# A gated linear attention with two MLPs: one prefix scan for all heads of a chunk, contiguous transposed copies, and part of the weight split on TensorE

## The chip, the cores and the metric

The kernel runs on one core of a Trainium2 chip. The metric is the device time of one launch in microseconds (us); three runs of the kernel before gave 1174.3, 1174.88 and 1174.89 us, median 1174.88. The profiled execution took 1172.15 us, of which the trace's span is 1170.1 us.

## The reference

A complex-valued recurrence per batch (4), head (8) and position (768), head size 48, then two MLPs over the 3072 tokens, everything in fp32:

```python
mag = np.sqrt(a_re * a_re + a_im * a_im)
scale = np.minimum(mag, 0.999) / (mag + 1e-06)
a_re_n, a_im_n = a_re * scale, a_im * scale
for t in range(S):
    ar, ai = a_re_n[:, :, t, :, None], a_im_n[:, :, t, :, None]
    new_re = ar * S_re - ai * S_im
    new_im = ar * S_im + ai * S_re
    S_re, S_im = new_re + np.einsum('bhd,bhe->bhde', k[:, :, t], v[:, :, t]), new_im
    y[:, :, t] = np.einsum('bhd,bhde->bhe', q[:, :, t], S_re)
x = y.transpose(0, 2, 1, 3).reshape(3072, 384)
x = np.maximum(x @ w_in, 0.0) ** 2 @ w_out                 # w_in 384x2048, w_out 2048x384
g = x @ w_gate
out = (g / (1 + np.exp(-g)) * (x @ w_val)) @ w_out2        # 384x1536, 384x1536, 1536x384
```

## The kernel before

The sequence is cut into six chunks of 128 positions; with the batch of 4 a chunk has 512 tokens. For every chunk there are three pieces of work.

**Attention** (`attention`, `elem`, `mat`). The eight heads are four groups of two. `elem` works in the layout 128 partitions = 4 batches x 32 blocks of positions, each block of 4 positions (`nb`) in the free dimension. It loads the decays (`load`, names `in2`, shown as `in`), normalises them with Ln and Exp on ScalarE (`sq`, `lg`, `b0`, `z`), and forms running complex products on VectorE: within a block of 4 (`an`, through the scratch `AB`), then over the 32 blocks by a five-level scan in a transposed copy `X`. The result `gb` multiplies `an` to give the prefix products `pp` (scratch `Bt`). With them q and k are scaled to `qs` and `ks`. All of this runs once for each pair of groups (`m`, twice a chunk). `mat` transposes `ks` and `qs` on TensorE into PSUM (`pt`), copies them to `kT`, `qT` with ScalarE, makes scores (`sc`), masks them (`pb`), applies them to v (`py`) and updates the `state` (`pu`, `rho`). `pt` is written in contiguous runs; the copy to `kT`/`qT` puts elements 4 apart.

**First MLP** (`moe1`): 16 steps, each 9 matmuls into `h` and, two steps later, 9 into `acc`; an fp32 number is the sum of two fp32r numbers, and each product is three matmuls (high times high, high times low, low times high). ScalarE makes `u` and `gh`, VectorE makes `gl`. **Second MLP** (`moe2`): 12 steps a chunk with `pg`, `pv`, `acc`, after all chunks of the first.

**Weights.** `prep1` loads 32 tiles of `w_in` and `w_out`, `prep2` 36 tiles of the second MLP (`wst`). `wsplit` builds the fp32 value with three VectorE instructions (`wt`), ScalarE casts the high part (`wc`, `wr`), VectorE subtracts to get the low part, and ScalarE takes two checks of the original bits (`wst<-wst`).

**Order.** All calls between `constants` and `issue` go through `Plan`: `record` keeps each call with its dependences, `arrange` runs a list schedule with estimated durations (`weigh`), in which the rank of an instruction is its place in the recorded program, and `issue` emits the calls in that order on the five in-order engines. So every instruction shows the line of one helper in the profile, and groups are told apart by tile names. `fast` sets the recorded order: attention of chunk 0 first, then `moe1` of chunk n interleaved with the attention of chunk n+1 (`drain`, weights `NATT`), with `prep1` run between the steps of `moe1(0)` (`behind`).

Of the kernel before, what the change touches and what calls it, by code (L numbers as in the profile page):

```python
# [22 lines left out]
class Op:  # L23
    __slots__ = ("call", "args", "kw", "engine", "step", "last", "after", "order", "users", "need", "frees", "tiles", "rank",
                 "ready", "pair", "size")
# [13 lines left out]
class Plan:  # L39
# [9 lines left out]
    def __init__(self, tc):  # L49
        self.tc, nc = tc, tc.nc  # L50
        self.ops, self.seen, self.slots, self.tags = [], {}, {}, {}
        for name in ("tensor", "vector", "scalar", "sync", "gpsimd"):
            setattr(self, name, Engine(self, getattr(nc, name), name))

    @staticmethod
    def region(ap):
        (row, parts), free = ap.ap[0], ap.ap[1:]
        if ap.space == bass.MemoryType.DRAM:
            return 0, 1, ap.offset, ap.offset + sum(st * (n - 1) for st, n in ap.ap) + 1
        p, f = divmod(ap.offset, row)  # L60
        return p, p + parts, f, f + sum(st * (n - 1) for st, n in free) + 1
# [8 lines left out]
    def record(self, engine, method, call, args, kw):  # L70
# [4 lines left out]
        o = Op()  # L75
        i = len(self.ops)
        o.call, o.args, o.kw, o.engine, o.rank = call, args, kw, engine, i
        o.after, o.order, o.users, o.frees, o.tiles, o.ready, o.pair, o.size = set(), set(), [], [], [], 0.0, None, 0
        self.ops.append(o)
        for k, ap in aps.items():  # L80
# [11 lines left out]
            for j, r, w in t[1]:  # L92
                if (write or w) and j != i and r[0] < at[1] and at[0] < r[1] and r[2] < at[3] and at[2] < r[3]:
                    same = self.ops[j].engine == engine and engine != "sync"
# [4 lines left out]
                    if write and at[0] <= r[0] and r[1] <= at[1] and at[2] <= r[2] and r[3] <= at[3] and j not in o.order:  # L99
                        continue  # L100
# [10 lines left out]
    def weigh(self, engine, method, full, aps):  # L111

        out = aps["out"]
        n = self.width(out)
        if engine == "vector":
# [26 lines left out]
        parts = out.ap[0][1] if out.space != bass.MemoryType.DRAM else aps["in_"].ap[0][1]  # L142
        free = out if out.space != bass.MemoryType.DRAM else aps["in_"]
        return 470, 2000 + 4 * parts * self.width(free) / 200.0


    def arrange(self):
# [38 lines left out]
        while len(result) < n:  # L186
# [45 lines left out]
            if e == "tensor":  # L232
# [9 lines left out]
                if o.pair and lastpair and o.pair[0] == lastpair[0] and o.pair[1] != lastpair[1]:  # L242
                    now[e] -= 0
                    step *= 0.06
                lastpair = o.pair
                acc += step
            if e in ("sync", "gpsimd"):
# [34 lines left out]
class Kern:  # L282
    CHUNKS = None

    NIN = 3
    NPP = 3
# [7 lines left out]
    NATT = 150  # L294
# [6 lines left out]
    READ = 8  # L301

    LOADS = 5
# [3 lines left out]
    def __init__(self, tc, q, k, v, a_re, a_im, w1, w2, wg, wv, wo, out):  # L307
# [8 lines left out]
        self.G, self.SG = 2, 2  # L316
# [3 lines left out]
        for nb in self.CHUNKS or [4] * (self.S // 128):  # L320
            self.chunks.append((t, nb))
            t += 32 * nb
# [3 lines left out]
    def pools(self, ctx):  # L326
# [11 lines left out]
        self.wbufs, self.wlive, self.wspare = self.WBUFS, 0, []  # L338
        self.x2, self.in2 = {}, {}

    def constants(self, ctx):
# [28 lines left out]
        self.ytile = c.tile([128, self.SG * W // 32, 32], F32, name="ytile")  # L370
        nc.vector.memset(self.ytile, 0.0)

    def flags(self, pool):
# [8 lines left out]
        self.low = pool.tile([128, n * NG // self.SG, self.SG * self.G * self.D // 32], F32, name="low")  # L382
# [34 lines left out]
    def load(self, n, g, names):  # L417
# [4 lines left out]
        t = self.ld.tile([128, 2, G, nb * D], F32, name="in2", tag="in2", bufs=self.NIN)  # L422
# [14 lines left out]

    def cmul(self, o, x, y, AB):

        nc = self.nc  # L440
        w = list(x.shape[2:])
        nc.vector.tensor_tensor(out=AB, in0=x.unsqueeze(1).to_broadcast([128, 2, 2] + w),
                                in1=y.unsqueeze(2).to_broadcast([128, 2, 2] + w), op=ALU.mult)
# [3 lines left out]
    def elem(self, n, m, res):  # L447

        nc, G, D, W, SG = self.nc, self.G, self.D, self.W, self.SG
        t0, nb = self.chunks[n]  # L450
        NG = self.H // G
        VW = SG * W
        big = lambda nm: self.e2.tile([128, 2, nb, W], F32, name=nm, tag="pp", bufs=self.NPP)
        smn = lambda nm: self.e2.tile([128, nb, W], F32, name=nm, tag="smn", bufs=self.NSMN)
        sml = lambda nm: self.e2.tile([128, nb, W], F32, name=nm, tag="smk", bufs=self.NSMK)
        cs = lambda nm, shape: self.e2.tile(shape, F32, name=nm, tag="cs", bufs=6)
        perm = lambda t: t.rearrange("p h (r d) -> p r h d", r=nb)
        v4 = lambda t: t.rearrange("p r (h d) -> p r h d", h=G)
        an = self.e2.tile([128, 2, nb, VW], F32, name="an", tag="an", bufs=1)
        part = lambda i: an[:, :, :, i * W:i * W + W]  # L460

        for i in range(SG):
            a2 = self.load(n, m * SG + i, (self.a_re, self.a_im))
            sq = [smn(f"sq{c}") for c in range(2)]
# [5 lines left out]
            lg = smn("lg")  # L470
# [3 lines left out]
            b0 = smn("b0")  # L474
# [11 lines left out]
            for c in range(2):  # L486
                nc.vector.tensor_tensor(out=v4(part(i)[:, c]), in0=perm(a2[:, c]), in1=v4(sc), op=ALU.mult)
# [8 lines left out]
        X = self.e2.tile([128, 2 * K * 32 + 32], F32, name="X", tag="X", bufs=1)  # L496
        X4 = lambda t: t.rearrange("p (c k j) -> p c k j", c=2, k=K)
        bs = slice(m * K, (m + 1) * K)
        for c in range(2):
            nc.vector.transpose(out=X[:, 32 * K * c + 1:32 * K * (c + 1) + 1], in_=an[:, c, nb - 1])  # L500
        t31 = cs("t31", [128, 2, K])
        nc.vector.tensor_copy(t31, X4(X[:, 32:])[:, :, :, 0])
# [597 lines left out]
```

## Time and profile before

| what | value |
| --- | --- |
| median of three runs | 1174.88 us |
| profiled execution | 1172.15 us |
| its span | 1170.1 us |
| TensorE busy (matmul) | 1054.8 us, 90% |
| VectorE busy | 728.9 us, 62% |
| ScalarE busy | 656.2 us, 56% |
| mean granted clock of TensorE | 0.972 |

Busy times are unions over the span; the launch takes 2.05 us more than the span. An engine's share says little here, since the kernel has three stages with different limits, so the stretches are read one by one.

### The profile page before, as it was taken

The numbers are of one execution on the slowest core, as the hardware profiler recorded it, in microseconds if no ns is written. First come the engines' busy times: TensorE is split into PE (matmuls) and PEld (weight loads), VectorE is DVE, ScalarE is ACT, GpSimd is POOL, SyncE is SP. The second block draws the span as 40 slices with busy tenths as digits, with TensorE's granted clock in tenths as the row PEclk, the third lists the DMA queues.
The fourth block names the chain that finished last, engine by engine and source line by source line (L and its number), as shares of the span: only waits on it lengthen the run. The fifth ranks groups of instructions, "written<-read, shape, count | busy, mean of one in ns | idle before, by whom it ended". The sixth has DMA issues, their size and how long they took to land.

```text
span 1170.1 us, 16337 instructions
## 1 busy us (share of the span) xinstructions
PE 1054.8 (90%) x5842; PEld 892.8 (76%) x5842; DVE 728.9 (62%) x1582; ACT 656.2 (56%) x1332; POOL 0.9 (0%) x7
## 2 busy tenths in 40 slices
PE   0527586989999999999999999999999999999997
PEld 0425465768888888888888788888888888888886
DVE  6998999798969879886886787522232222322221
ACT  2657687987678776777767998522122221311211
POOL 0000000000000000000000000000000000000000
PEclk9958897999999999999999999999999999999999
DMA  5426345223141432414224545110010010000000
GB/s 174 135 62 170 109 137 147 71 79 92 46 130 60 109 102 62 122 48 129 73 50 138 187 134 177 55 41 13 1 55 1 7 48 1 28 1 1 28 1 31
DMA packets 102490, 89.25 MB, mean 76 GB/s; under 512 B 35072, under 2 KB 90368, under 8 KB 102400
## 3 DMA queue, kind: packets, MB, share of 16 engines
q1 hardware_dynamic: 102400, 88.12, 25.6%
q8 instruction: 48, 0.79, 0.3%
q14 instruction: 42, 0.34, 0.1%
HBM read 64.49 MB, written 18.87 MB: 71 GB/s over the span
## 4 chain that ended last, share of the span: by engine, by line
PE 77%; ACT 10%; DVE 9%; issue 1%; DMA 1%; SPq 1%; DVEq 0%; ACTq 0%
PE acc L279 25%; PE pg L279 13%; PE pv L279 13%; PE h L279 12%; PE py L279 4%; PE pt L279 3%; PE sc L279 3%; ACT wst L279 3%; PE pu L279 3%; DVE AB L279 1%; ACT u L279 1%; DVE wt L279 1%; SPq L279 1%; DVE pp L279 1%; ACT gh L279 1%
## 5 line engine op out<-in xcount | busy, mean ns | idle before, releaser
L279 ACT CAST gh<-u 128x512 fp32r<-128x512 f32 x168 | 103.9, 619 | 220.2 <-PE acc L279 195.0
L279 PE MATMUL h<-xh,wc 128*128 128x512 f32 x576 | 203.5, 406 | 25.7 <-ACT wc L279 19.9
L279 PE MATMUL acc<-gh,wr 128*128 128x512 f32 x576 | 202.2, 406 | 6.9 <-ACT gh L279 6.9
L279 DVE TENSOR_TENSOR gl<-u,gh 128x512 fp32r<-128x512 f32 x168 | 115.7, 689 | 117.5 <-ACT gh L279 116.7
L279 DVE TENSOR_TENSOR u<-pv,u 128x512 f32<-128x512 f32 x72 | 49.7, 691 | 191.9 <-PE pv L279 189.6
L279 PEld LDWEIGHTS h<-xh,wc 128*128 128x128 f32 x576 | 109.2, 192 | 52.6 <-ACT wc L279 21.8
L279 PE MATMUL acc<-wr,gh 128*128 128x384 f32 x576 | 147.3, 336 | 0.0
L279 PE MATMUL pg<-xh,wc 128*128 128x512 f32 x432 | 145.9, 392 | 0.0
L279 PE MATMUL pv<-xh,wc 128*128 128x512 f32 x432 | 144.9, 390 | 0.0
L279 PEld LDWEIGHTS acc<-gh,wr 128*128 128x128 f32 x576 | 108.8, 192 | 30.6 <-ACT gh L279 9.6
L279 PE MATMUL h<-xl,wc 128*128 128x512 f32 x288 | 116.0, 403 | 2.2 <-DVE xl L279 2.2
L279 PE MATMUL acc<-gl,wr 128*128 128x512 f32 x288 | 115.6, 402 | 0.3 <-DVE gl L279 0.2
L279 PEld LDWEIGHTS acc<-wr,gh 128*128 128x128 f32 x576 | 105.6, 188 | 4.7
L279 ACT ACTIVATE u<-pg 128x512 f32<-128x512 f32 x72 | 43.0, 598 | 98.2 <-PE pg L279 97.6
L279 PE MATMUL acc<-wr,gl 128*128 128x384 f32 x288 | 97.1, 337 | 0.0
L279 PEld LDWEIGHTS pv<-xh,wc 128*128 128x128 f32 x432 | 81.2, 188 | 17.3
L279 PEld LDWEIGHTS pg<-xh,wc 128*128 128x128 f32 x432 | 81.2, 188 | 15.5
L279 PE MATMUL pt<-ident,ks 128*96 128x128 f32 x192 | 31.3, 288 | 64.5 <-DVE ks L279 63.5
L279 PE MATMUL pg<-xl,wc 128*128 128x512 f32 x216 | 85.1, 394 | 0.0
L279 PE MATMUL pv<-xl,wc 128*128 128x512 f32 x216 | 84.3, 390 | 0.0
L279 ACT ACTIVATE u<-h 128x512 f32<-128x512 f32 x96 | 57.1, 595 | 40.7 <-PE h L279 38.3
L279 PEld LDWEIGHTS pt<-ident,ks 128*96 128x96 f32 x192 | 22.9, 135 | 68.4 <-issue 64.4
(111 smaller groups left out, 1820.2 us busy)
## 6 DMA issues: line engine op xcount, KB each, us to landing
wst<-in_moe_w_out_dram SPq DMA_DIRECT2D x28, 384.0 KB, 3.5
scr<-ks SPq DMA_DIRECT2D x24, 384.0 KB, 2.6
kn<-scr SPq DMA_DIRECT2D x24, 384.0 KB, 3.7
wst<-in_moe_w_in_dram SPq DMA_DIRECT2D x16, 384.0 KB, 4.7
in<-in_a_re_dram SPq DMA_DIRECT2D x96, 48.0 KB, 1.9
in<-in_a_im_dram SPq DMA_DIRECT2D x96, 48.0 KB, 1.9
in<-in_k_dram SPq DMA_DIRECT2D x96, 48.0 KB, 2.8
in<-in_q_dram SPq DMA_DIRECT2D x96, 48.0 KB, 2.6
```

The costliest lines, as they stand in the source:

```text
L279: o.call(*o.args, **o.kw)
```

## The change

It has seven parts.

1. **One scan for a chunk.** `elem` handles all four groups at once. The tile `X` doubles to 768 columns, and the five scan levels run once a chunk with operands twice as wide. `an` becomes one resident tile `[128, 2, 4, 384]`.
2. **Prefix products by another route.** Before, three chained complex products a pair of groups gave the products within a block, and then all four positions were multiplied by `gb`. Now the products are 0·1 and 2·3, then 01·23 for the scan; after it positions 0 and 1 are multiplied by the scanned prefix, position 2 by the new position 1, and position 3 is not multiplied at all: it is the scan shifted by one column, transposed back straight into `an[:, :, 3]`. A complex product (`cmul`) is one 768-wide and two 192-wide instructions.
3. **Strided transposition.** The TensorE transposes write `pt` with a step of 4 elements, so the copy to `kT` and `qT` is contiguous.
4. **Subtraction on TensorE.** For the first `BYPE` = 16 tiles of `prep1` the low part is `ident`·x − `ident`·high, two matmuls of 384 columns (fp32 with `ident`, fp32r with the new `nident`) into a PSUM tile `pw`, and a ScalarE cast from there.
5. **Loads.** A tile `in2` takes 4 DMAs of 96 KB (128 partitions, one head each) in place of 8 of 48 KB (32 partitions). The pattern on the DRAM side is 4 batches x 32 blocks x 192 numbers. For chunk 0 all decays are loaded first, some from ScalarE's queue, into free weight buffers.
6. **Chunk 0 and the weights.** Attention 0 takes its PSUM tiles from all eight banks; `prep1` reads 2 tiles ahead instead of 8 and is recorded with a later rank (`late`), 4 steps for 100 of the attention.
7. **The planner** keeps exact regions of strided tiles and adds an estimated cost for TensorE's change between the narrow matmuls and the others.

```diff
 # elem
-        for s in range(1, nb):
-            AB = self.e2.tile([128, 2, 2, VW], F32, name="AB", tag="cm", bufs=1)
-            self.cmul(an[:, :, s], an[:, :, s - 1], an[:, :, s], AB)
+            if i % 2:
+                for r in (0, 2):
+                    self.cmul(an[:, :, r + 1, cols(i - 1, 2)], an[:, :, r, cols(i - 1, 2)], an[:, :, r + 1, cols(i - 1, 2)], 2 * W)
...
+        for i in range(0, NG, 2):
+            self.cmul(an[:, :, 3, cols(i, 2)], an[:, :, 1, cols(i, 2)], an[:, :, 3, cols(i, 2)], 2 * W)
...
-        nc.vector.transpose(out=gb.rearrange("p c w -> p (c w)"), in_=X)
+        for c in range(2):
+            nc.vector.transpose(out=an[:, c, 3], in_=X[:, 32 * K * c:32 * K * (c + 1)])
+        nc.vector.tensor_copy(after, last)
...
-            nc.vector.tensor_tensor(out=f3(pp), in0=f3(part(i)), in1=bg(0), op=ALU.mult)
-            nc.vector.tensor_tensor(out=f3(Bt), in0=f3(part(i)), in1=bg(1), op=ALU.mult)
...
-            nc.vector.tensor_tensor(out=pp[:, 0], in0=pp[:, 0], in1=Bt[:, 1], op=ALU.subtract)
-            nc.vector.tensor_tensor(out=pp[:, 1], in0=pp[:, 1], in1=Bt[:, 0], op=ALU.add)
+            if i % 2 == 0:
+                for r in range(2):
+                    self.cmul(an[:, :, r, cols(i, 2)], an[:, :, r, cols(i, 2)], an[:, :, 3, cols(i, 2)], 2 * W)
...
+                self.cmul(an[:, :, 2, cols(i, 2)], an[:, :, 1, cols(i, 2)], an[:, :, 2, cols(i, 2)], 2 * W)
...
+                for c in range(2):
+                    nc.vector.transpose(out=an[:, c, 3, cols(i, 2)], in_=X0[:, 32 * K * c + i * W + 1:][:, 0:2 * W])
 # load
-        for b in range(B):
-            for c, src in enumerate(names):
-                nc.sync.dma_start(out=t[32 * b:32 * b + 32, c], in_=src[b, h0:h0 + G, t0:t0 + 32 * nb, :].rearrange(
-                    "h (j r) d -> j h (r d)", r=nb))
+        for c, src in enumerate(names):
+            for h in range(G):
+                q = nc.scalar if n == 0 and g < 2 and h and src is not self.q and src is not self.k else nc.sync
+                q.dma_start(out=t[:, c, h], in_=src[:, h0 + h, t0:t0 + 32 * nb, :].rearrange("b (j r) d -> b j (r d)", r=nb))
 # mat
-                    nc.tensor.transpose(pt[:, rr].rearrange("p b j -> p (b j)"),
+                    nc.tensor.transpose(pt.rearrange("p (x r) -> p r x", r=nb)[:, rr],
                                         src[:, rr, h].rearrange("p c d -> p (c d)"), self.ident)
-                nc.scalar.copy(dst[:, h].rearrange("p b (j r) -> p r b j", r=nb), pt)
+                nc.scalar.copy(dst[h], pt)
 # wsplit
-        nc.vector.tensor_tensor(out=dst[:, 1], in0=x, in1=dst[:, 0].bitcast(F32), op=ALU.subtract)
+        if pe:
+            pw = self.ps.tile([128, 384], F32, name="pw", tag="ps")
+            nc.tensor.matmul(pw, self.ident, x, start=True, stop=False)
+            nc.tensor.matmul(pw, self.nident, dst[:, 0], start=False, stop=True)
+            nc.scalar.copy(dst[:, 1], pw)
+        else:
+            nc.vector.tensor_tensor(out=dst[:, 1], in0=x, in1=dst[:, 0].bitcast(F32), op=ALU.subtract)
 # fast
-        for _ in range(self.LOADS):
-            next(first)
+        next(first)
         next(w1)
-        drain((first, NATT))
+        drain((first, NATT), (self.late(w1, 1000), self.WITH), until=first)
```

How the instructions stand now is shown at three places. First VectorE, where the scan of chunk 0 begins (`wt` is a weight tile, `X` the transposed scan). Before:

```order
L279 TENSOR_TENSOR AB<-an 128x768
L279 TENSOR_TENSOR an<-AB 128x192 x2
L279 STREAM_TRANSPOSE X<-an 128x192 x2
L279 COPY t_142<-X 128x12
L279 COPY X<-phase 128x12
L279 TENSOR_TENSOR AB<-X 128x192 x2
L279 TENSOR_TENSOR X<-AB 128x96 x2
```

And of the change:

```order
L306 TENSOR_SCALAR wt<-wst 128x384
L306 TENSOR_TENSOR AB<-an 128x768
L306 SCALAR_TENSOR_TENSOR wt<-wst,wt 128x384
L306 TENSOR_TENSOR an<-AB 128x192 x2
L306 SCALAR_TENSOR_TENSOR wt<-wst,wt 128x384
L306 TENSOR_TENSOR AB<-an 128x768
L306 TENSOR_TENSOR an<-AB 128x192 x2
L306 STREAM_TRANSPOSE X<-an 128x384 x2
```

The scan is twice as wide and starts later in the queue, behind all four groups' normalisation; three weight tiles' `wt` now stand ahead of it, the third of them between the last products, where before no weight work stood.

Second TensorE, at its first instructions in the program (`pr` is a small matmul for `rho`). Before, row one is the first transposition:

```order
L279 MATMUL pt<-ident,ks 96x128 x4
L279 MATMUL pt<-ident,qs 96x128 x4
L279 MATMUL pt<-ident,ks 96x128 x4
L279 MATMUL pt<-ident,qs 96x128 x4
L279 MATMUL pr<-ident,ysrc 96x4 x2
L279 MATMUL sc<-qT,kT 128x128 x8
```

Of the change, from the first instruction, and further down at the end of attention 0:

```order
L306 MATMUL pw<-wt,ident 128x384
L306 MATMUL pw<-wc,nident 128x384
L306 MATMUL pr<-ident,ysrc 96x4 x2
L306 MATMUL pt<-ident,ks 96x128 x4
...
L306 MATMUL pu<-vt,kn 96x48 x7
L306 MATMUL pw<-wr,nident 128x384
L306 MATMUL pw<-wc,nident 128x384
L306 MATMUL h_305<-xh,wc 128x512
```

The subtractions now stand among the attention's and the first MLP's matmuls, and the first `h` follows when the attention of chunk 0 is through, where before `h` and attention 0 were mixed.

Third SyncE's DMA queue at the start of the program. Before:

```order
L279 DMA in_124<-in_a_re_dram 32x2x192
L279 DMA in_124<-in_a_im_dram 32x2x192
L279 DMA wst<-in_moe_w_in_dram 128x3x256
L279 DMA wst<-in_moe_w_out_dram 128x768
L279 DMA wst<-in_moe_w_in_dram 128x3x256
```

And of the change:

```order
L306 DMA in_123<-in_a_im_dram 128x1x192 x2
L306 DMA wst<-in_moe_w_in_dram 128x3x256
L306 DMA wst<-in_moe_w_out_dram 128x768
L306 DMA vt<-in_v_dram 128x4x48 x4
L306 DMA in_142<-in_k_dram 128x1x192 x2
L306 DMA in_142<-in_q_dram 128x1x192 x2
...
L306 DMA in_145<-in_q_dram 128x1x192 x2
L306 DMA wst<-in_moe_w_in_dram 128x3x256
```

The third weight tile, the one whose `wt` stands ahead of the scan, is now issued behind all loads of k, q and v of chunk 0: 12 decay loads, two tiles, 4 of v and 16 of k and q stand ahead of it.

## Rows read from the trace of the kernel before

**Rows 1.** The page, part 2: busy tenths in 40 slices of the span.
```profile
PE   0527586989999999999999999999999999999997
DVE  6998999798969879886886787522232222322221
```

**Rows 2.** Windows: stretch, its length, busy time (instructions) by engine, clock, DMA share, GB/s.
```profile
0.00:25.00 25.00, 0.00 (x0) 0.00 (x0) 14.34 (x41) 8.06 (x15) 0.94 (x7) 1.00 0.61 184
25.00:112.00 87.00, 40.38 (x291) 32.74 (x291) 76.42 (x181) 54.74 (x110) 0.00 (x0) 0.83 0.47 129
112.00:252.00 140.00, 108.78 (x611) 84.66 (x612) 125.42 (x290) 113.36 (x270) 0.00 (x0) 0.88 0.37 108
275.00:625.00 350.00, 350.00 (x2233) 293.38 (x2232) 287.76 (x659) 260.25 (x477) 0.00 (x0) 1.00 0.32 90
625.00:725.00 100.00, 98.25 (x512) 79.92 (x511) 75.87 (x153) 90.86 (x227) 0.00 (x0) 1.00 0.52 162
```

**Rows 3.** Tile gl on VectorE up to 256 us: duration, first and last start.
```profile
L279 DVE TENSOR_TENSOR gl<-u,gh x16: 672/688/694, 112.0 to 251.9; 128x512 fp32r<-128x512 f32 x16
```

**Rows 4.** Groups on VectorE, whole span: busy us, mean ns of one, idle before.
```profile
L279 DVE TENSOR_TENSOR AB<-X 128x192 f32<-128x192 f32 x120 | 37.7, 352 | 1.0
L279 DVE TENSOR_TENSOR X<-AB 128x96 f32<-128x96 f32 x120 | 25.4, 252 | 0.9
L279 DVE TENSOR_TENSOR AB<-an 128x768 f32<-128x768 f32 x36 | 34.4, 955 | 0.9
L279 DVE TENSOR_TENSOR pp<-an,gb 128x768 f32<-128x768 f32 x24 | 22.8, 952 | 0.0
L279 DVE TENSOR_TENSOR pp<-pp,Bt 128x384 f32<-128x384 f32 x48 | 25.1, 545 | 0.1
L279 DVE STREAM_TRANSPOSE X<-an 128x192 f32<-128x192 f32 x24 | 7.6, 355 | 0.0
L279 DVE STREAM_TRANSPOSE gb<-X 128x384 f32<-128x384 f32 x12 | 6.9, 571 | 0.0
L279 DVE TENSOR_TENSOR wc<-wt,wc 128x384 fp32r<-128x384 f32 x40 | 22.1, 554 | 9.5 <-ACT wc L279 9.5
```

**Rows 5.** Groups on ScalarE, whole span.
```profile
L279 ACT COPY qT<-pt 96x512 f32<-96x512 f32 x48 | 54.5, 1136 | 0.0
L279 ACT COPY x<-acc 128x512 f32<-128x512 f32 x18 | 9.7, 587 | 2.8 <-PE acc L279 2.5
L279 ACT COPY o<-acc 128x384 f32<-128x384 f32 x12 | 5.8, 480 | 19.3 <-PE acc L279 19.3
```

**Rows 6.** TensorE's timeline near 475 us: start, length, instructions merged.
```profile
475.52 0.60 PE L279 MATMUL pt<-ident,ks 128*96 128x128 f32 x4
475.96 0.60 PE L279 MATMUL pt<-ident,qs 128*96 128x128 f32 x4
...
477.88 0.48 PE L279 MATMUL acc<-gl,wr 128*128 128x512 f32 x1
478.20 0.39 PE L279 MATMUL acc<-gh,wr 128*128 128x512 f32 x1
...
479.95 1.95 PE L279 MATMUL sc<-qT,kT 96*128 96x128 f32 x16
```

**Rows 7.** The chain that ended last, one piece of the second MLP: start, length.
```profile
732.56 2.10 PE acc L279 x12
```

**Rows 8.** SyncE's first issue; windows of DMA; its packets from 2 to 9 us.
```profile
0.82 0.40 SPq L279 DMA_DIRECT2D in<-in_a_re_dram  x1
...
2.00:9.00 7.00, 0.00 (x0) 0.00 (x0) 0.56 (x1) 2.90 (x8) 0.00 (x0) 1.00 0.39 104
...
16.00:17.00 1.00, 0.00 (x0) 0.00 (x0) 0.97 (x3) 0.00 (x0) 0.00 (x0) 1.00 1.03 394
...
DMA packets 1190, 0.73 MB, mean 104 GB/s; under 512 B 240, under 2 KB 1190, under 8 KB 1190
...
wst<-in_moe_w_in_dram SPq DMA_DIRECT2D x1, 384.0 KB, 4.0
```

More of the change, by code (lines that the diff above doesn't have):

```diff
@@ L76, in record @@
         i = len(self.ops)
-        o.call, o.args, o.kw, o.engine, o.rank = call, args, kw, engine, i
-        o.after, o.order, o.users, o.frees, o.tiles, o.ready, o.pair, o.size = set(), set(), [], [], [], 0.0, None, 0
+        o.call, o.args, o.kw, o.engine, o.rank = call, args, kw, engine, i + self.later
+        o.after, o.order, o.users, o.frees, o.tiles, o.ready, o.pair = set(), set(), [], [], [], 0.0, None
+        o.dma = method == "dma_start"
         self.ops.append(o)
@@ L92, in record @@
             for j, r, w in t[1]:
-                if (write or w) and j != i and r[0] < at[1] and at[0] < r[1] and r[2] < at[3] and at[2] < r[3]:
-                    same = self.ops[j].engine == engine and engine != "sync"
+                if (write or w) and j != i and self.meet(r, at):
+                    same = self.ops[j].engine == engine and not o.dma and not self.ops[j].dma
                     if same and (not w or engine == "tensor"):
@@ L98, in record @@
                         o.after.add(j)
-                    if write and at[0] <= r[0] and r[1] <= at[1] and at[2] <= r[2] and r[3] <= at[3] and j not in o.order:
+                    if write and j not in o.order and self.within(r, at):
                         continue
@@ L114, in weigh @@
         n = self.width(out)
+        if method == "dma_start":
+            free = out if out.space != bass.MemoryType.DRAM else aps["in_"]
+            return 470, 2000 + 4 * free.ap[0][1] * self.width(free) / 200.0
         if engine == "vector":
@@ L141, in weigh @@
             return step, step + 190
-        parts = out.ap[0][1] if out.space != bass.MemoryType.DRAM else aps["in_"].ap[0][1]
-        free = out if out.space != bass.MemoryType.DRAM else aps["in_"]
-        return 470, 2000 + 4 * parts * self.width(free) / 200.0
+        assert False, (engine, method)
     def arrange(self):
@@ L457, in elem, with two @@
         perm = lambda t: t.rearrange("p h (r d) -> p r h d", r=nb)
         v4 = lambda t: t.rearrange("p r (h d) -> p r h d", h=G)
[L459 to L464, printed above, removed]
+        an = self.an
+        cols = lambda i, k=1: slice(i * W, (i + k) * W)
+        def two(a, b):
+            if n:
+                return smn(a), smn(b)
+            t = self.wp.tile([128, 2, nb, W], F32, name=a, tag="w", bufs=self.wbufs)
+            return t[:, 0], t[:, 1]
@@ new lines, in out @@
+        def out(name, shape):
+            if n:
+                return self.e2.tile(shape, F32, name=name, tag=name, bufs=1)
+            return self.wp.tile(shape, F32, name=name, tag="w", bufs=self.wbufs)
+        decay = {}
+        for i in range(NG):
+            if n == 0 and i == 0:
+                decay = {j: self.load(n, j, (self.a_re, self.a_im)) for j in range(NG)}
+                yield
+            a2 = decay.pop(i, None) or self.load(n, i, (self.a_re, self.a_im))
+            sq = two("sq0", "sq1")
@@ L684, in wtile @@
             pool, tag, bufs = self.wspare.pop(0)
+            if tag == "an":
+                if self.four is None:
+                    self.four = pool.tile([128, 4, 2, 3, 128], F32R, name=nm, tag=tag, bufs=bufs)
+                return self.four[:, len(self.wspare)]
             return pool.tile([128, 2, 3, 128], F32R, name=nm, tag=tag, bufs=bufs)
@@ L732, in prep1 @@
                 _, _, i, name, dst = todo[j]
-                self.convert(name, read[j], i, dst)
+                self.convert(name, read[j], i, dst, ahead > 0, ahead > 0 and j < self.BYPE)
             yield
@@ L881, in elems @@
         def elems():
-            for m in range(NG // self.SG):
-                yield from self.elem(n, m, res)
+            yield from self.elem(n, res)
         def mats():
@@ L946, in fast, with late @@
             drain((self.moe2(n), 24))
+    def late(self, it, by):
+        while True:
+            self.nc.later = by
+            step = next(it, it)
+            self.nc.later = 0
+            if step is it:
+                return
+            yield
     @staticmethod
```

200 lines of the change are left out of this document (120 added, 80 removed).

## The prediction

> **What bounds the kernel now.** I read the slices of the page first. TensorE's row is full from the tenth slice on and ragged before, while VectorE's row is full at the start and thin at the end [rows 1]. The windows say the same in numbers: from 275 to 625 us TensorE is busy for 350.00 of 350 us, with VectorE at 287.76 and ScalarE at 260.25; before 252 us TensorE has 149.2 of 252 us, VectorE 216.2 [rows 2]. So what VectorE or ScalarE saves after 275 us buys nothing, and what is added to TensorE there is paid in full. The time can come from the first 252 us: the 16th `gl`, the last VectorE step of chunk 0's first MLP, starts at 251.9 us [rows 3], and by then all 32 weight tiles are split and the attention of chunk 1 is through. VectorE is idle for only 35.8 us up to there: 10.7 in the first 25 us, where it waits for loads, 10.6 up to 112 us, where the first `gl` starts, and 14.6 in the 140 us after. In that last stretch it is busy for 90%, ScalarE for 81% and TensorE for 78% at a granted clock of 0.88 [rows 2]. VectorE sets the pace, with the other two not far behind.
>
> **VectorE, up to the 16th gl.** Instructions overlap a little at their ends, so I price one by a group's busy time over its count. The 16 subtractions that leave cost 22.1/40 = 0.553 us each [rows 4]: −8.9. The rest is worked out for a chunk. Scan: 20 `AB<-X` at 0.314 and 20 `X<-AB` at 0.212 were 10.5 us; now 10 of 384 columns and 10 of 192, priced by the 384-column `pp<-pp` (0.523) and the 192-column `AB<-X`, are 8.4: −2.1. Prefix multiplication: 4 `pp` and 4 `Bt` alike at 0.95 and 8 `pp<-pp` at 0.523 were 11.8 us; six complex products at 0.956 + 2 × 0.314 = 1.58 are 9.5: −2.3. Transpositions grow: 4 of 192 columns (0.317) and 2 of 384 (0.575) were 2.4 us, now 4 of each are 3.6: +1.2. `ks` becomes two of 384 for one of 768, 4 × (1.05 − 0.95): +0.4. The products inside a block stay six a chunk; six small instructions a chunk that go are left out. Together −2.8 us a chunk, and two chunks lie up to the mark: −5.6 [rows 4]. Counting the emitted order at these durations shows one thing more: ahead of the 16th `gl` the queue held the normalisation of two groups of chunk 2, and now a little over one, with fewer of its products: about −3 us. That work is not saved but falls into the stretch where VectorE has 62 us of slack in 350 [rows 2]. So −17.5 us in all, of 216.
>
> **ScalarE** gains and loses. A copy of `pt` with scattered output took 1.136 us, a plain one of 512 columns from PSUM 0.587 [rows 5]: 16 a chunk, −8.8 us. The 16 casts from `pw` cost about 0.48 each by the 384-column copy [rows 5]: +7.7. After the first `gl` these cancel, and ScalarE stays at about 112 of the stretch's time.
>
> **TensorE in that stretch.** The first matmul of a subtraction is fp32: `sc`, 16 instructions for 8 products of 128 columns, ends after 1.95 us, 0.24 us each [rows 6], so 384 columns take some 0.73. The second is fp32r, 12 of 384 columns in 2.10 us, 0.175 [rows 7]. Sixteen pairs: 14.5 us. The cover is the 103 us that TensorE idles before 252 us [rows 2]; without it, all 14.5 us would be paid. TensorE's 108.8 us in the 140 at clock 0.88 are about 96 at full clock, so with the pairs it needs some 111.
>
> So the stretch after the first `gl` has three engines at about 110 us: VectorE 125.4 − 8.9 − 2.8 − 3 = 111, ScalarE 112, TensorE 111. With the utilisation that VectorE has now, 0.90, it takes 112/0.90 = 125 in place of 140 us: −15. Ahead of it, one chunk's saving of 2.8 is partly eaten by the three weight tiles' `wt` that now stand before the scan, while the four groups' loads, all issued at the start, should fill some of the 10.7 us of early idleness; I take −3 net, between −8 (both come through) and +6 (the wider chain delays the first `ks`, on which TensorE waits until attention 0 can begin). The new waits are two: VectorE waits for the third `wst` with the whole scan queued behind it, and TensorE's second `pw` matmul waits for a ScalarE cast, with scores and `h` behind it.
>
> **After the mark.** TensorE has by the emitted order about 3 us less of its other work behind it at the end of chunk 0's first MLP (+3). It returns from narrow fp32 matmuls to the wide ones 73 times in chunks 1 to 5, before 89; such a return costs about 0.1 us, the step of 0.32 us behind a transposition against the 0.23 that 512 columns take at the pace of the second MLP [rows 6, 7]: −1.6. From 625 to 725 us only 1.75 us of TensorE are idle [rows 2]; earlier weight tiles may give one back.
>
> The strided transposition is priced from both sides. Four transpositions take 0.44 us, 0.11 each, that is 0.86 ns for each of 128 columns; a fp32r matmul puts out its 384 columns in 0.175 us, 0.46 ns a column [rows 6, 7]. The transposition thus writes PSUM at half the pace that the same engine reaches with contiguous output, and a strided write has as much again to spare. That speaks for nothing, the lower end. The upper end is what ScalarE pays when its output is scattered by the same 16 bytes: (1.136 − 0.587)/512 = 1.07 ns an element [rows 5], 0.137 us a transposition, 35 us for the 256 of chunks 2 to 5. I take 0, nearest to the pace of the transposition itself. [...]
>
> **The sum** against the profiled execution: 1172.15 − 3 − 15 + 3 − 1.6 − 1 = 1154.6 us. The runs shown have a median 2.7 us above that execution, so **1157 us**.
>
> **The rivals.**
> *Narrow loads.* In every DMA of the kernel before, the outermost step counts 16 or a multiple of it, and the small packets say that all 16 engines took part: 240 in a stretch with 15 issues [rows 8]. The new loads have 4 batches outermost on the DRAM side. If only 4 engines serve them, then at 104 GB/s for 39% of 16 engines, 16.7 GB/s an engine, 96 KB take 1.47 us; at the 394 GB/s of a full stretch 1.0 [rows 8]. The third weight tile waits behind 32 such loads: 1.3 + 32 to 47 + 4 to land, 37 to 52 us, where VectorE could need it at about 30; it loses 7 to 22 us with the scan behind it, 16 in the middle: 1173. For it speaks the pattern, against it that nothing here shows a transfer so confined. [...]
>
> *Three engines out of step.* If the utilisation falls to 0.84 because each now waits for the others, the stretch takes 133 us, and the first part gains nothing: 1168. For it speaks that VectorE now stands 12 us above the next engine in that stretch [rows 2] and that after the change the three stand within 1 us; against it, that less work waits in each queue.
>
> *Strided writes are slow* (the other side). At the ScalarE price 1157 + 35 = 1192; it decides from 0.07 us a transposition on, where 256 eat the 18 us.
>
> *The gain is smaller than a measurement can tell*: narrow loads at their lower end together with neither step lost gives 1164, so this needs the narrow loads at their middle, above.
>
> **Chances.** As summed 0.50, own range 1148 to 1164; narrow loads 0.25; out of step 0.15; slow writes 0.10. The range from 1146 to 1179 leaves out the slow writes and the far ends of the first two. A measurement tells some 0.2%, 2.3 us, from no change. Faster: all of the first, most of the third, half of the second: 0.76. Same, 1172.5 to 1177.2: 0.10. Slower: 0.14.
>
> **What would show it.** Right: the 16th `gl` starts near 234 us; TensorE stays full from there to 625; four `pt` still take 0.44 us; copies to `kT` near 0.59; VectorE idles less than 10 us in the first 25. Wrong: `wt` waits for a DMA ahead of the scan, loads of 96 KB that land late and leave 4 small packets in place of 16; `pt` above 0.15 us; `h` waiting for `pw`'s casts, with VectorE idle for more than 20 us between the first and the 16th `gl`.

## The result, and the profile after

The changed kernel takes 1186.27 us (median of 4 runs, 1183.56 to 1189.98) against 1174.64 us before: a ratio of 1.0101, 95% interval 1.0071 to 1.0131. The forecast was 1157, range 1146 to 1179, so the kernel became slower where it should have become faster. The profiled execution took 1184.89 us, its span is 1182.7 us.

The slices of the page, TensorE and VectorE:

```profile
PE   0056979999999999999999998999999999999997
DVE  3896898879879878888957796222232222322222
```

The windows of [rows 2]:

```profile
0.00:25.00 25.00, 0.00 (x0) 0.00 (x0) 6.08 (x22) 8.64 (x18) 0.94 (x7) 1.00 0.40 113
25.00:112.00 87.00, 34.69 (x232) 28.67 (x232) 68.94 (x157) 41.05 (x94) 0.00 (x0) 0.92 0.30 91
112.00:252.00 140.00, 124.74 (x713) 98.22 (x712) 123.10 (x274) 118.14 (x296) 0.00 (x0) 0.91 0.47 141
275.00:625.00 350.00, 344.39 (x2226) 289.37 (x2225) 289.97 (x623) 232.60 (x469) 0.00 (x0) 0.99 0.32 95
625.00:725.00 100.00, 98.58 (x485) 80.64 (x481) 82.17 (x171) 93.53 (x246) 0.00 (x0) 1.00 0.49 149
```

VectorE is busy for 6.08 of the first 25 us, before 14.34, and TensorE is no longer full from 275 to 625 us: 344.39 of 350, before 350.00. Against that, TensorE is busy 16 us longer in the stretch from 112 to 252. The tile `gl`, as in [rows 3]:

```profile
L306 DVE TENSOR_TENSOR gl<-u,gh x16: 674/688/695, 134.2 to 249.4; 128x512 fp32r<-128x512 f32 x16
```

The first `gl` starts 22 us later than before, the 16th 2.5 us earlier (forecast: 18 earlier), and the rest behind the 16th lasts 933.3 us instead of 918.2. So the kernel gains 25 us between the first and the 16th `gl`, loses 22 of them at the start, and loses 15 us more behind the 16th, where the forecast had next to nothing.

The groups on VectorE, ScalarE and TensorE that answer to [rows 4, 5] (busy us, mean ns, idle before):

```profile
L306 DVE TENSOR_TENSOR AB<-X 128x384 f32<-128x384 f32 x60 | 31.0, 554 | 0.7
L306 DVE TENSOR_TENSOR X<-AB 128x192 f32<-128x192 f32 x60 | 18.9, 355 | 0.6
L306 DVE TENSOR_TENSOR AB<-an 128x768 f32<-128x768 f32 x72 | 68.6, 952 | 0.8
L306 ACT COPY qT<-pt 96x512 f32<-96x512 f32 x48 | 27.9, 582 | 4.1 <-PE pt L306 4.0
L306 PE MATMUL pw<-wt,ident 128*128 128x384 f32 x32 | 16.3, 595 | 33.5 <-DVE wt L306 33.5
L306 PE MATMUL pw<-wc,nident 128*128 128x384 f32 x8 | 4.1, 512 | 8.4 <-ACT wc L306 8.4
L306 ACT CAST wc<-pw 128x384 fp32r<-128x384 f32 x8 | 3.8, 475 | 0.8 <-PE pw L306 0.8
```

The prices hold: 0.52 and 0.315 us for the wide scan (forecast 0.523 and 0.314), 0.58 for the contiguous copy (0.587), 0.475 for the cast (0.48). Only TensorE's pairs cost more by their groups, about 1.5 us each, (16.3 + 4.1 + 4.0)/16 with the eight of `wr`, for a forecast of 0.9. The transpositions, as in [rows 6]:

```profile
78.99 0.60 PE L306 MATMUL pt<-ident,qs 128*96 128x128 f32 x4
79.42 0.60 PE L306 MATMUL pt<-ident,ks 128*96 128x128 f32 x4
79.86 0.60 PE L306 MATMUL pt<-ident,qs 128*96 128x128 f32 x4
```

Four still take 0.43 to 0.44 us, with strided output. What does not hold is the loads. SyncE's queue at the start (start, length, transfers merged):

```profile
13.41 2.01 SPq L306 DMA_DIRECT2D in<-in_a_im_dram  x2
15.47 0.96 SPq L306 DMA_DIRECT2D wst<-in_moe_w_in_dram  x1
...
30.30 2.01 SPq L306 DMA_DIRECT2D in<-in_q_dram  x2
32.36 2.01 SPq L306 DMA_DIRECT2D in<-in_k_dram  x2
34.42 2.27 SPq L306 DMA_DIRECT2D in<-in_q_dram  x2
36.73 0.96 SPq L306 DMA_DIRECT2D wst<-in_moe_w_in_dram  x1
```

In such a row a narrow load (96 KB, outermost step of 4) takes SyncE 1.0 us, where the first old one of 48 KB took 0.40 [rows 8]. Over the first 50 us, the view of the DMA engines (busy tenths and GB/s in 40 slices of this window, then packets):

```profile
DMA  0022222222222499963122222222224822000000
GB/s 0 10 39 90 93 93 93 92 93 93 93 92 93 122 301 335 237 163 68 56 90 93 92 93 93 93 92 93 93 93 119 297 88 83 15 7 0 0 0 0
DMA packets 7282, 4.74 MB, mean 95 GB/s; under 512 B 2288, under 2 KB 7152, under 8 KB 7280
```

While narrow loads run alone, the mean busy share of the 16 engines is about a quarter (digit 2; 0.27 from 5 to 14 us) and 93 GB/s pass, though more loads stand in the queue. By my estimate that is four engines at 23 GB/s each, near the 394/16 = 24.6 of the full stretch before [rows 8]. 96 KB at 93 GB/s are 1.06 us, the pace of the issues. And the wait that the forecast named as the sign of it is there, on VectorE's timeline (third weight tile, then the scan):

```profile
43.59 0.36 DVE L306 TENSOR_SCALAR wt<-wst 128x384 int32<-128x384 int32 x1 [3.60 <-DMA wst<-in_moe_w_in_dram]
...
47.74 1.03 DVE L306 STREAM_TRANSPOSE X<-an 128x384 f32<-128x384 f32 x2
```

### The profile page after: what moved, and what is told of

The parts are those of the page before. It is cut to its first block, busy times and chain, and to the rows that moved or that the text cites. A ratio compares the mean times of both kernels' runs of the same rounds, so it can differ in the third digit from the quotient of the medians.

```text
span 1182.7 us, 16112 instructions
## 1 busy us (share of the span) xinstructions
PE 1071.8 (91%) x5890; PEld 905.4 (77%) x5890; DVE 705.6 (60%) x1452; ACT 615.6 (52%) x1331; POOL 0.9 (0%) x7
## 4 chain that ended last, share of the span: by engine, by line
PE 70%; ACT 10%; DVE 9%; DMA 6%; SPq 3%; issue 2%; ACTq 0%; DVEq 0%
PE acc L306 23%; PE pv L306 13%; PE pg L306 13%; PE h L306 11%; ACT wst L306 3%; SPq L306 3%; PE py L306 3%; PE pt L306 3%; PE sc L306 3%; PE pu L306 2%; DVE AB L306 2%; ACT u L306 2%; DVE wt L306 1%; DMA in<-in_a_im_dram 1%; DVE an L306 1%
## 5 line engine op out<-in xcount | busy, mean ns | idle before, releaser
L306 PE MATMUL h<-xh,wc 128*128 128x512 f32 x576 | 200.6, 403 | 3.6 <-ACT u L306 1.9
L306 PE MATMUL acc<-gh,wr 128*128 128x512 f32 x576 | 198.2, 399 | 0.2 <-ACT gh L306 0.2
L306 PE MATMUL pv<-xh,wc 128*128 128x512 f32 x396 | 133.8, 392 | 2.6 <-ACT u L306 2.6
L306 PE MATMUL pg<-xh,wc 128*128 128x512 f32 x396 | 135.0, 394 | 1.1 <-ACT xh L306 1.1
L306 PEld LDWEIGHTS pv<-xh,wc 128*128 128x128 f32 x396 | 74.3, 188 | 19.6 <-ACT u L306 3.0
L306 PEld LDWEIGHTS pg<-xh,wc 128*128 128x128 f32 x396 | 74.3, 188 | 16.2 <-ACT xh L306 1.5
L306 PE MATMUL pg<-xl,wc 128*128 128x512 f32 x198 | 78.2, 395 | 0.1
L306 PE MATMUL pv<-xl,wc 128*128 128x512 f32 x198 | 77.7, 393 | 0.0
L306 DVE SCALAR_TENSOR_TENSOR wt<-wst,wt 128x384 int32<-128x384 int32 x136 | 74.7, 554 | 1.9
L306 DVE TENSOR_TENSOR AB<-an 128x768 f32<-128x768 f32 x72 | 68.6, 952 | 0.8
```

The source lines that it names most:

```text
L306: o.call(*o.args, **o.kw)
```

## The experiments

Theories at the start: the narrow loads cost the time; or the wider scan and the weights ahead of it do; later, whether the transfers cost it or the order that the planner makes of them. The kernel before was run beside each; its medians lay between 1172.6 and 1177.3 us, so ratios are compared, and 0.001 of ratio is 1.2 us. Intervals are 95%.

**The loads of the kernel before, in all chunks, in the first alone, in the others alone; and the narrow loads alone in the kernel before.**

```diff
 # load
+        if True:                      # or: if n == 0 / if n > 0
+            for b in range(B):
+                for c, src in enumerate(names):
...
+                    q.dma_start(out=t[32 * b:32 * b + 32, c], in_=src[b, h0:h0 + G, t0:t0 + 32 * nb, :].rearrange(
+                        "h (j r) d -> j h (r d)", r=nb))
+            return t
```

> The changed kernel with the k, q, v and decay loads of the kernel before (eight transfers of 48 KB for each tensor of a chunk, rows of a head to 32 partitions), all else as changed. Narrow loads: the transfers that run on 4 of the 16 DMA engines set the late start, so the first gl comes back from 134 us to about 110 to 113 and the time to 1155 to 1167 us. Rival (the longer start is the scan over all heads and the whole-weights work ahead of it on VectorE, whatever the loads): the first gl stays past 125 and the time at 1180 or more.

> As the changed kernel, but chunk 0 alone has the loads of the kernel before. Narrow loads: the start has all or nearly all of the loss, so the first gl is at 110 to 114 us and the time 1158 to 1170. If the later chunks' narrow loads cost as much as the start (waits for kn past 300 us), it gives less: 1170 to 1178. Rival (scan and weights ahead): 1180 or more.

> As the changed kernel, but the chunks after the first alone have the loads of the kernel before; chunk 0 keeps the narrow ones. Narrow loads at the start: first gl stays near 134 us, and only the few us of waits for kn past 300 us come back: 1176 to 1185 us. If the narrow loads hurt through the later chunks' transfers that lie beside the start, the first gl comes down and the time is below 1172.

> The kernel before with one edit, the narrow loads (96 KB for each head pair of a batch, 16 partitions) in place of its own. Narrow loads: it is slower than the kernel before by 10 to 25 us (1185 to 1200), the first gl at 122 to 135 us in place of 112. Rival (loads are hidden behind the weights and attention): within 4 us of the kernel before.

The narrow loads put into the kernel before are those of the change: each has one head of all four batches on 128 partitions, and not, as the last text says, a head pair of one batch on 16.

| loads | ratio | interval |
| --- | --- | --- |
| changed kernel, narrow | 1.0101 | 1.0071 to 1.0131 |
| old loads in all chunks | 0.9848 | 0.9816 to 0.9881 |
| old loads in chunk 0 alone | 1.0012 | 0.9995 to 1.0030 |
| old loads behind chunk 0 alone | 0.9923 | 0.9895 to 0.9951 |
| kernel before with narrow loads | 1.0611 | 1.0572 to 1.0651 |

With the old loads the changed kernel takes 1157.19 us. All of the loss and more was the loads: 0.0253, 30 us. But two expectations were wrong. The start has the smaller share: 0.0089 (10 us) comes back with chunk 0's loads alone, 0.0178 (21 us) with the later ones. And the first `gl` does not return to 112. The tile `gl` of the kernel with the old loads:

```profile
L306 DVE TENSOR_TENSOR gl<-u,gh x16: 675/685/694, 125.7 to 231.5; 128x512 fp32r<-128x512 f32 x16
```

Its windows up to the first `gl` and from there to the 16th:

```profile
0.00:125.70 125.70, 46.38 (x313) 37.25 (x314) 100.99 (x231) 64.35 (x146) 0.95 (x7) 0.95 0.44 120
125.70:231.50 105.80, 101.86 (x623) 81.87 (x622) 95.17 (x215) 100.66 (x257) 0.00 (x0) 0.98 0.50 145
```

VectorE now does more of its work ahead of the first `gl` (100.99 us, before 90.76), so the first stretch is longer and the second shorter; the 16th `gl`, at 231.5, is what counts. Behind it the kernel with the old loads takes 923.5 us: of the 15 us lost there, 10 are the loads', and 5 stay, which no run takes apart. Its view of the DMA engines, first 50 us:

```profile
DMA packets 8178, 4.74 MB, mean 95 GB/s; under 512 B 3184, under 2 KB 8048, under 8 KB 8176
```

There are 896 more small packets than in the changed kernel for the same bytes. Chunk 0 has 32 narrow loads, or 64 old ones: 64 × 16 − 32 × 4 = 896. If each engine that takes part leaves one small packet, each narrow load ran on 4 engines and each old one on 16. The share of about a quarter fits that. No view shows the engines one by one, so "four engines" and "16 engines" below stand for this reading of packets and share.

In the kernel before, the narrow loads cost 72 us, far more than the 10 to 25 expected: its 16th `gl` starts at 266.6 us, 15 later, and the other 57 us lie behind it. TensorE there waits nine times for `kn`, the keys that come back from DRAM for the state update, and in the kernel before not once:

```profile
PE pu L279 <- DMA kn<-scr: 20.9, 9, 4.1
```

That is 20.9 us in all, 4.1 at the longest. Why that order suffers so much more than the changed one was not taken apart.

**Transfers or order.** The planner counts 0.47 us of SyncE for any load, and half as many loads make another order. Two kernels keep one order and issue the other transfers in it; a third tells the planner 1.0 us.

```diff
 # load, in the order made for narrow loads (the other kernel does the reverse)
+                def wide(out, in_, raw=o.call, c=c, src=src, h=h):
+                    for b in (2 * h, 2 * h + 1):
+                        raw(out=t[32 * b:32 * b + 32, c], in_=src[b, h0:h0 + G, t0:t0 + 32 * nb, :].rearrange(
+                            "h (j r) d -> j h (r d)", r=nb))
+                o.call = wide
 # weigh (third kernel)
+            if free.ap[0][1] == 128 and self.width(free) == 192:
+                return 1000, 3000
```

> The changed kernel with its order of instructions kept on all five engines as the planner made it with the narrow loads, but each narrow transfer of 96 KB is issued as two transfers of 48 KB with 32 partitions, which spread over 16 DMA engines. It tells the transfers themselves from the order that the planner makes of them. If the transfers alone cost the 29 us between the changed kernel and its version with the old loads: 1155 to 1163 us. If the loss is the order that the planner makes when it counts half as many issues: 1180 or more. If both, in between, and the distance from 1157 is the share of the order.

> The other half of that pair: the order that the planner makes for the old loads (1157 us with these), but the transfers that are issued in it are the narrow ones, two of 96 KB in place of four of 48. Transfers alone: 1182 to 1190 us. Order alone: 1155 to 1162. Both: in between, and this distance from 1157 is the share of the transfers.

> The changed kernel, narrow loads kept, but the planner counts 1.0 us of SyncE and of DMA for each (the issues of the changed kernel stand 1.0 us apart) where it had 0.47 us and a transfer of 0.49. If the loss comes from an order built on wrong durations, the planner puts weights and the rows of kn ahead and 8 to 20 us come back (1166 to 1178). If the transfers cost it whatever the order, it stays at 1180 to 1190.

| order made for | narrow transfers | transfers on 16 engines |
| --- | --- | --- |
| narrow loads | 1.0101 | 0.9972 (0.9946 to 0.9997) |
| old loads | 1.0093 (1.0063 to 1.0123) | 0.9848 |

Told of 1.0 us, the planner gets 0.9983 (0.9963 to 1.0003). So with narrow transfers the order made no difference (0.0008); with spread ones it is worth 0.0124, 15 us. The transfers cost 15 us in one order and 29 in the other. Both theories hold in part, and the two do not add. My reading is that an order is only worth something if the transfers keep to the times it was made for. A planner that knows the slow loads wins back 14 of the 30 us.

The 15 us between the two orders are not the order's alone. In the order made for narrow loads, two old loads stand in the place of one narrow load, and SyncE takes longer over them than the 0.47 us that the planner counted. SyncE's timeline of that kernel:

```profile
78.64 1.83 SPq L467 DMA_DIRECT2D in<-in_a_im_dram  x4
```

Four take 1.83 us, a pair 0.92, nearly as long as one narrow load. So the upper row of the table is the cleanest test of the engines: order and queue are kept, SyncE's time for the same bytes is nearly the same, and the spread over 16 engines alone brings 15 us.

**Queue or engines.** Do the narrow loads cost because others stand behind them in SyncE's queue, or because four engines are behind? First the loads went out from GpSimd's queue (GpSimd is busy for 0.9 us of the span), order kept:

```diff
...
+                if q is nc.sync:
+                    nc.ops[-1].call = self.tc.nc.gpsimd.dma_start
```

> The changed kernel with its order of instructions and its narrow transfers, but those that SyncE issued go out from GpSimd's DMA queue, GpSimd being idle in this kernel. Nothing else moves. If the narrow transfers cost because kn, scr and the weights stand in SyncE's one queue behind transfers that keep 4 engines busy for 1.0 us each: the 16 us between 1186 and 1170 (same order, spread loads) come back in most part, 1168 to 1177. If the cost is that the loaded q, k and decays themselves land late: 1181 to 1192. If GpSimd's issues are slower than SyncE's: above 1192.

> The order that the planner makes for the old loads, narrow transfers in it (1186 with SyncE's queue, 1157 with the old transfers), again with the narrow transfers from GpSimd's queue. Queue: 1158 to 1170. Late landing of the loads themselves: 1180 to 1190.

> The changed kernel with the loads of the kernel before (48 KB, 16 engines; 1157 us with SyncE's queue), of which those of SyncE go out from GpSimd's queue; order kept. If SyncE's queue holds back kn, scr and weights with spread loads too (it issues one every 0.43 us): 1148 to 1155. If the queue only costs with transfers on 4 engines: 1155 to 1160. If GpSimd issues them more slowly than SyncE, so that the decays of chunk 0 come late: 1161 or more.

Ratios 0.9894 (0.9866 to 0.9921) in the order made for narrow loads, 0.9908 (0.9873 to 0.9943) in the other, and 0.9837 (0.9818 to 0.9856) with the old loads. Taken alone this speaks for the queue. But the first kernel's view of the DMA engines from 20 to 28 us shows something else:

```profile
DMA packets 1115, 1.05 MB, mean 131 GB/s; under 512 B 812, under 2 KB 918, under 8 KB 1115
## 3 DMA queue, kind: packets, MB, share of 16 engines
q0 software_dynamic: 1045, 0.98, 54.7%
```

GpSimd's narrow loads alone (0.98 of 1.05 MB) take a share of 55% of the 16 engines, where SyncE's kept about a quarter busy. A share of 55% needs more than four engines, so these runs moved two things at once; which engines they were, no run here shows. With spread loads in the order made for them, moving the queue brings 0.0011, which can't be told from nothing: 1153.79 us is the fastest kernel of this study, but not measurably faster than the one with the old loads.

The queue is not without effect, though. From GpSimd's queue the two orders come out alike (0.9894 and 0.9908), and in the order made for narrow loads the 0.9894 lies 0.0078 (9 us) under the 0.9972 of spread loads in SyncE's queue. So part of the 15 us between the orders was time in SyncE's queue.

Next the narrow loads stayed in SyncE's queue and the others were moved to GpSimd's: `scr` and `kn`; these and the weights; everything. The last as an edit:

```diff
 # issue
+                if o.dma and o.engine == "sync" and o.pair != "load":
+                    o.call = self.tc.nc.gpsimd.dma_start
...
 # load
+                nc.ops[-1].pair = "load"
```

> The changed kernel, its order kept, its narrow loads left in SyncE's queue; the 24 pairs of scr and kn alone go out from GpSimd's queue, so that they no longer stand behind narrow loads that take SyncE 1.0 us each. Queue (what stands behind the narrow loads is late): the waits of pu for kn, 8.4 us in all, go, and 5 to 15 us come back (1171 to 1181). Engines (the four engines are behind, so that the loads themselves, and whatever else needs these four, land late from any queue): 1183 to 1190.

> As the run beside it, and the weight tiles of both MLPs go out from GpSimd's queue too: the third no longer stands behind 32 loads of k, q and v. SyncE keeps the narrow loads, x and the output. Queue: the third weight tile is there before the scan, the scan starts up to 4 us earlier (the wait for that tile is 3.6 us now), and with the waits for kn 8 to 20 us come back (1166 to 1178). Engines: 1183 to 1190. If the loads of the decays alone, which stand ahead of everything, set the scan: no earlier scan, and less than 8 us back.

> The changed kernel, its order kept; SyncE's queue holds the narrow loads alone, and every other transfer that it issued (weights, scr, kn, v, ys and x, the output) goes out from GpSimd's queue. Queue: nothing stands behind a narrow load any more, 10 to 20 us come back (1166 to 1177). Engines (the four engines are behind for all that needs them, from any queue): 1183 or more, scr and kn still 5 us to landing where they took 2.6 and 3.7 us before. GpSimd's own issues, 0.75 us each where SyncE took 0.36, make it a little slower in either case.

Ratios 1.0131 (1.0085 to 1.0177), 1.0146 (1.0094 to 1.0199), 1.0098 (1.0061 to 1.0136): nothing comes back. In the last kernel SyncE's queue holds narrow loads alone, and the transfers from GpSimd's still land late (KB, median us from issue to landing):

```profile
wst<-in_moe_w_out_dram POOLq DMA_DIRECT2D x28, 384.0 KB, 4.9
scr<-ks POOLq DMA_DIRECT2D x24, 384.0 KB, 5.7
kn<-scr POOLq DMA_DIRECT2D x24, 384.0 KB, 4.3
```

The kernel before had 3.5, 2.6 and 3.7 us for the three, from SyncE's queue. Part of the difference may be GpSimd's queue: in the first 50 us old loads of 48 KB land after 2.0 to 3.6 us from it, and after 1.9 from SyncE's; how 384 KB fare in it beside old loads, no run shows. The reading that fits is that a transfer on all 16 engines is late as long as narrow loads keep four of them busy; which engine a late transfer waited for, no view shows. But landing late is not the loss itself. In the kernel with the narrow loads on GpSimd's queue, 24 us faster than the changed one, `scr` still takes 4.3 us to land and `kn` 3.9:

```profile
scr<-ks SPq DMA_DIRECT2D x24, 384.0 KB, 4.3
kn<-scr SPq DMA_DIRECT2D x24, 384.0 KB, 3.9
```

So standing in a queue behind narrow loads does not by itself explain the loss: freeing the others of it brings nothing, and spreading the loads with queue and order kept brings 15 us. As I read it, that leaves the four engines as the main cause, with the queue as an addition in one of the two orders. How much of the 15 to 29 us is late decays, k and q, and how much is late `kn`, `ys` and weights, stays open.

**The other parts of the change**, each undone in the kernel with the old loads (0.9848), and the strided transposition alone in the kernel before.

```diff
 # no subtraction on TensorE
-    BYPE = 16
+    BYPE = 0
 # contiguous transposition (alone in the kernel before: the reverse)
-                    nc.tensor.transpose(pt.rearrange("p (x r) -> p r x", r=nb)[:, rr],
+                    nc.tensor.transpose(pt.rearrange("p (r x) -> p r x", r=nb)[:, rr],
...
-                nc.scalar.copy(dst[h], pt)
+                nc.scalar.copy(dst[h].rearrange("p (x r) -> p r x", r=nb), pt.rearrange("p (r x) -> p r x", r=nb))
 # no weights in attention 0
-        drain((first, NATT), (self.late(w1, 1000), self.WITH), until=first)
+        drain((first, NATT))
 # 8 tiles read ahead
-    READ = 2
+    READ = 8
```

> Old loads, and all subtractions of the weights on VectorE again (no pw). Prediction's account: 16 subtractions of 0.553 us come back on VectorE, which paces the stretch up to the 16th gl, while TensorE loses 14.5 us of pairs that lay in idle time and ScalarE 7.7: the 16th gl later by 9 to 10 us at a utilisation of 0.90, the time 1163 to 1168. Rival (the pairs cost TensorE as much as they save VectorE, since TensorE's idle time before the mark is short after the change): 1154 to 1159.

> Old loads, and the transpositions write pt in contiguous runs again, with the scattered copy on ScalarE (16 a chunk, 0.55 us more each by the groups of ScalarE). If strided writes are free, as the four-transposition steps of 0.44 us say: ScalarE becomes the slowest of the three engines between the first and the 16th gl (8.8 us more), so 5 to 10 us are lost up to the mark and 1162 to 1168 us come out. Rival (strided writes slow TensorE a little where it is full, in the chunks behind the mark): 1157 or less.

> The kernel before with this one edit: transpositions write pt with a step of 4 elements and the copy is contiguous. ScalarE gains 8.8 us a chunk, but VectorE paced the stretch: 1166 to 1175 us, and four pt still 0.43 to 0.45 us apart. Rival (strided writes slow): four pt above 0.5 us, 1175 or more.

> Old loads, and no weight tile is recorded inside the attention of chunk 0 (the third and later tiles follow it). If weights ahead of and in the scan delay the start: the scan and attention 0 come 2 to 5 us earlier, but their 4 tiles a 100 steps are work that has to be done before the 16th gl all the same, so the time stays within 1152 to 1160. Rival (this weight work fills idle time of VectorE and TensorE in attention 0): 1163 or more.

> Old loads, and the weights are read 8 tiles ahead, as in the kernel before, in place of 2, so that the third to eighth tile are issued ahead of k, q and v. If the third tile's late landing (its issue at 31 us) matters once the loads run on 16 engines: 1150 to 1156. If it is hidden: 1156 to 1160; if six tiles ahead of k and q delay ks: 1160 or more.

| kernel | ratio | interval | 16th `gl`, us |
| --- | --- | --- | --- |
| no subtraction on TensorE | 0.9956 | 0.9926 to 0.9985 | 242.5 |
| contiguous transposition | 0.9929 | 0.9906 to 0.9953 | 239.8 |
| before, strided transposition | 0.9941 | 0.9922 to 0.9959 | 247.6 |
| no weights in attention 0 | 0.9899 | 0.9865 to 0.9932 | 238.7 |
| 8 tiles read ahead | 0.9857 | 0.9822 to 0.9893 | 235.2 |

The subtraction on TensorE is worth 13 us and the strided transposition 10; from the three engines' sums 6 to 11 and 5 to 11 were expected, so the first lies a little above its range. Its rival, a slow strided write, falls: in the kernel before the same edit alone gains 7 us, and four transpositions there (its TensorE timeline) keep their pace:

```profile
415.05 0.60 PE L279 MATMUL pt<-ident,ks 128*96 128x128 f32 x4
415.49 0.60 PE L279 MATMUL pt<-ident,qs 128*96 128x128 f32 x4
```

So a step of 16 bytes in PSUM does not slow these fp32 transpositions: four stand 0.44 us apart, as with contiguous output [rows 6]. Weights in attention 0 are worth 6 us: without them the first `gl` comes at 111.7, as in the kernel before, but the 16th at 238.7:

```profile
L306 DVE TENSOR_TENSOR gl<-u,gh x16: 673/689/693, 111.7 to 238.7; 128x512 fp32r<-128x512 f32 x16
```

Here my expectation was wrong and its rival right: they fill idle time. Reading further ahead changes nothing that can be told.

## Why the prediction was wrong

- *The step that failed* is the price of the loads. The sum gave part 5 of the change nothing of its own: "the four groups' loads ... should fill some of the 10.7 us of early idleness; I take −3 net, between −8 ... and +6". Measured, the loads cost 30 us, a third of it by chunk 0's loads and two thirds by those of the later chunks. While they run alone they move 93 GB/s at a busy share of about a quarter. The early idleness grew too: VectorE is idle for 18.9 of the first 25 us, and with the old loads still for 14.7, before 10.7, so the loads filled none of it in either kernel. The first window with the old loads:

```profile
0.00:25.00 25.00, 1.62 (x2) 0.50 (x2) 10.33 (x31) 12.72 (x30) 0.95 (x7) 1.00 0.58 142
```

- *The rival that named it* had the mechanism as an "if", which the 896 fewer small packets and the share of about a quarter then bore out, and a quarter of the chance, and too small a size: 7 to 22 us (whose middle is 14.5, not 16), priced at one place, the third weight tile. The tile was there when it said, at 43.6 us (37 to 52), but VectorE came to it at 40.0 and not at 30, so it lost only 3.6 us waiting. Without that wait (weights on the other queue) the scan started at 41.9 instead of 47.7 and no time came back. The cost lay in what the rival left out: the other 160 loads, with 21 us, and the order that the planner made without knowing, worth 14 when it was told. VectorE's timeline without that wait:

```profile
41.94 1.03 DVE L306 STREAM_TRANSPOSE X<-an 128x384 f32<-128x384 f32 x2
```

- *The argument against it*, that nothing in the rows showed a transfer so confined, was no evidence: no transfer of the kernel before had an outermost step of 4, so no row could show one.
- *VectorE's term held.* Forecast −17.5 of 216.2 us up to the 16th `gl`, that is 198.7; measured 195.7 in the changed kernel (92.93 + 102.73 in two windows) and 196.2 with the old loads. The two windows:

```profile
0.00:134.20 134.20, 51.22 (x311) 40.76 (x312) 92.93 (x212) 64.04 (x145) 0.94 (x7) 0.92 0.38 114
134.20:249.40 115.20, 105.61 (x622) 83.95 (x621) 102.73 (x235) 101.62 (x259) 0.00 (x0) 0.93 0.43 131
```

- *The sum came out once the loads were taken out, in part by luck*: 1157.19 us for 1157, the 16th `gl` at 231.5 for 234, and 923.5 us behind it for 918.6. Its split did not: first `gl` forecast at 109, measured 125.7; the stretch to the 16th forecast 125 us, measured 105.8. The sum overlooked part 6 of the change: weight tiles split inside attention 0 hold up the first `gl` and leave less to do behind it. Without them the two are 111.7 and 127.0 us, near the forecast, and the time is 1165. So two errors of 17 and 19 us cancel up to the mark, and the 2.5 us left over there make up half of the 5 that the rest takes more than forecast.
- *Strided transposition at 0*: right, by the pace of four `pt` and by two runs. *TensorE's pairs*: hidden as forecast, though larger than priced: putting the subtractions back on VectorE costs 13 us.
- *Out of step* (utilisation 0.84): not seen. With the old loads VectorE is busy 90% of the stretch between first and 16th `gl` (95.17 of 105.8), TensorE 96%.

## What to carry to other kernels

Before pricing a rewritten transfer by its bytes, look at its outermost dimension: with a 4 there on the DRAM side, loads of 96 KB moved 93 GB/s at a busy share of about a quarter, and a row of them held SyncE's queue for 1.0 us each. When a planner or a written order sits on assumed durations, a change of durations must reach it: here 14 of 30 us came back by telling the planner, with no other edit. And a rival whose mechanism is visible in the code should be priced at every place where it acts, not at the first one.

## What the runs showed of the hardware that was not expected

- Narrow loads in GpSimd's queue ran at a larger share of the engines: 0.98 MB in 8 us, 122 GB/s at 0.55, where SyncE's had 92 GB/s at 0.27 (25 to 35 us of the changed kernel).
- SyncE's issues took longer beside narrow loads in GpSimd's queue: its first four of `vt` took 11.79 us, in the changed kernel 3.97, with the old loads 2.08. In all three kernels they stand directly behind the same two weight tiles; that the other queue's transfers are the cause is argued, not tested. The SyncE timeline of the kernel with narrow loads on GpSimd:

```profile
1.85 11.79 SPq L306 DMA_DIRECT2D vt<-in_v_dram  x4
16.22 0.37 SPq L306 DMA_DIRECT2D wst<-in_moe_w_in_dram  x1
```

- A fp32 transposition into PSUM with a step of 16 bytes kept its pace on TensorE, four in 0.44 us, and spared ScalarE 0.55 us a copy.
